# A decode layer on one core: the last PSUM copy and the output store moved to ScalarE

## The chip, the core and the metric

The kernel runs on one NeuronCore of a Trainium2 chip. The metric is the device time of one execution in microseconds (us), the lower the better. The core has five engines with instruction streams of their own: TensorE (PE in the profile, its weight loads PEld), VectorE (DVE), ScalarE (ACT), GpSimd (POOL) and SyncE (SP). SyncE and ScalarE both issue DMA transfers here; a transfer is issued by the engine's sequencer and then carried out by 16 DMA engines that all queues share. `ACTq` and `SPq` in the profile mean the sequencer of ScalarE and of SyncE.

## The reference

One decode step (batch 4, one token each) of a pre-norm transformer layer: attention over the last 2048 positions of a cache, then a gated MLP, both with residuals. Cut to what matters:

```python
# x: 4 x 1 x 1024; k_cache, v_cache: 4 x 4 x 8192 x 128; bf16 throughout
h  = x + attention(layernorm(x), k_cache, v_cache, wq, wo)   # 32 query heads, 4 kv heads
n  = layernorm(h)
h2 = h + (silu(n @ w1) * (n @ w3)) @ w2                      # 1024 -> 3584 -> 1024
return h2                                                    # 4 x 1 x 1024, bf16
```

## The kernel before

All weights and the cache go through one DMA queue, issued from SyncE in the order of use, into five rotating buffers. `w2` comes last, its second half in pieces of 5, 4, 2 and 1 rows, so that little work is left when the last byte arrives. The output is summed in one PSUM tile `y2_ps` of 128 partitions x 256 columns (fp32). Only 16 of its partitions are wanted: `JG` = 4 column blocks times 4 batch rows, `RS` = 8 partitions apart. The end of the kernel is a strict chain:

```python
    # SyncE has issued the last piece of w2 long before
    for i in range(IF):                                   # 28 row blocks of w2
        for j in range(JG):
            nc.tensor.matmul(
                y2_ps[QD * j : QD * (j + 1), :],
                lhsT=hgT[:, i, :],
                rhs=loaded["w2"][i][:, j * CG : (j + 1) * CG],
                start=False, stop=(i == IF - 1), skip_group_check=True,
            )

    res = act.tile([P, CG], BF16)
    nc.vector.tensor_copy(out=res[:], in_=y2_ps[:])                   # L440
    nc.sync.dma_start(                                                # L441
        out=out_flat.rearrange("b (j c) -> j b c", j=JG), in_=res[0:P:RS, :])
```

After this SyncE waits until all transfers have landed, one semaphore after another, and a barrier of all engines closes the program.

ScalarE's other DMA work are five small loads at the start: `x_sb` (4 rows of 1024) and four pieces of `x_q` (4 rows of 256).

## Time and profile before

The kernel before took 138.77 us (median of 3 runs, 138.73 to 138.95). The profiled execution's span, from first to last instruction, was 136.8 us.

| what | value | where it is read |
|---|---|---|
| HBM read | 55.59 MB, 406 GB/s over the span | HBM line of the page |
| DMA engines busy 90% or more | slices 2 to 36 of 40 | page, part 2 |
| last piece of `w2` landed | 133.11 us | chain of waits |
| last copy (VectorE) | 0.42 us | timeline |
| issue of the store (SyncE) | 0.69 us | timeline |
| wait for its landing (SyncE) | 1.1 us | waits of SyncE |

The page, kernel before. In the slice lines each digit is the busy share of a fortieth of the span, in tenths:

```profile
DMA  5999999999999999999999999999999999998950
...
HBM read 55.59 MB, written 0.01 MB: 406 GB/s over the span
```

So the kernel is bound by its stream of data for nearly the whole span, and what comes after 133 us is a tail that nothing overlaps.

The end of the chain that ended last, kernel before (start in us, duration in us, what):

```profile
95.73 37.38 DMA t<-in_B_w_dram
133.11 0.04 issue
133.15 0.32 PE y_ps L430 x4
133.49 0.42 DVE res L440
```

The timeline of the end, kernel before (start in us, duration in us, engine, line, operation, and in brackets the idle time before it and what ended it):

```profile
133.15 0.29 PE L430 MATMUL y_ps<-t,hgT 128*32 128x256 bf16 x4 [0.26 <-DMA t<-in_B_w_dram]
...
133.49 0.42 DVE L440 CAST res<-y_ps 128x256 bf16<-128x256 f32 x1 [11.29 <-PE y_ps L430]
133.94 0.69 SPq L441 DMA_DIRECT2D out_dram<-res  x1
```

The waits of SyncE at the end, kernel before (who waited for whom: total us, times, longest us). The store's landing takes 1.1 us after its issue:

```profile
SPq L467 <- DMA out_dram<-res: 1.1, 1, 1.1
```

The copies that ScalarE made before, in the groups of instructions (line, engine, operation, tiles, shapes, count, then busy us and mean ns of one):

```profile
L267 ACT COPY kT<-kt_ps 128x1024 bf16<-128x1024 bf16 x16 | 15.8, 1014 | 12.0 <-PE kt_ps L261 12.0
...
L318 ACT COPY bc<-bc_ps 128x128 f32<-128x128 f32 x1 | 0.3, 265 | 1.2 <-PE bc_ps L314 1.2
```

### The profile page before, as it was taken

Reading aid. Unit: us, or ns where it says so; the run is one execution under the profiler, and the core shown is the slowest. Engines: PE = TensorE matmul, PEld = TensorE weight load, DVE = VectorE, ACT = ScalarE, POOL = GpSimd, SP = SyncE. Lnnn points to the kernel's source line nnn. Section 1 sums busy time; section 2 is a strip of 40 time slices with the busy share of each in tenths; the row PEclk is TensorE's granted clock in tenths of the full one; section 3 lists DMA queues with packets and bytes.
Section 4 is the critical chain, followed back from the end, with each engine's and each line's share of the span. In section 5 each row is a group of like instructions: output and inputs, shape, how many; then the busy total and the mean of one; then the engine's idle time right before and its main releaser. Section 6 shows DMA issues by size and latency. Waiting matters only on the chain.

```text
span 136.8 us, 2307 instructions
## 1 busy us (share of the span) xinstructions
PE 68.3 (50%) x1035; PEld 42.3 (31%) x1035; DVE 43.0 (31%) x74; ACT 30.6 (22%) x35; POOL 1.7 (1%) x8
## 2 busy tenths in 40 slices
PE   0152303698989899105259259825080530802950
PEld 0110001274756565000149247602030210301820
DVE  6440000244444444709940030260004970170001
ACT  0400000155555646092943000000015000000000
POOL 5000000000000000000000000000000000000000
PEclk9999999999999999965555865896555586555586
DMA  5999999999999999999999999999999999998950
GB/s 156 441 418 503 402 393 441 421 431 436 421 431 421 436 436 417 433 445 469 450 421 402 407 427 441 453 441 402 427 449 453 411 419 424 450 460 364 418 219 2
DMA packets 3237, 55.74 MB, mean 407 GB/s; under 512 B 376, under 2 KB 408, under 8 KB 668
## 3 DMA queue, kind: packets, MB, share of 16 engines
q1 hardware_dynamic: 3188, 55.58, 95.2%
q8 instruction: 8, 0.13, 0.3%
q10 hardware_dynamic: 40, 0.02, 0.1%
q14 instruction: 1, 0.01, 0.0%
HBM read 55.59 MB, written 0.01 MB: 406 GB/s over the span
## 4 chain that ended last, share of the span: by engine, by line
DMA 43%; PE 29%; ACT 13%; DVE 8%; issue 4%; SPq 1%; ACTq 0%; DVEq 0%
DMA t<-in_B_w_dram 27%; DMA t<-in_A_wq_dram 15%; PE kt_ps L261 9%; ACT kT L267 6%; PE scores_ps L246 5%; PE OT_ps L324 5%; PE y_ps L351 4%; ACT z L302 3%; PE q_ps L213 2%; DVE rmax L278 2%; PE g_ps L400 2%; ACT Pm L283 2%; SPq L95 1%; DVE pT L292 1%; DVE z L298 1%
## 5 line engine op out<-in xcount | busy, mean ns | idle before, releaser
L267 ACT COPY kT<-kt_ps 128x1024 bf16<-128x1024 bf16 x16 | 15.8, 1014 | 12.0 <-PE kt_ps L261 12.0
L261 PE MATMUL kt_ps<-ident,t 128*128 128x128 bf16 x256 | 16.5, 220 | 0.0
L261 PEld LDWEIGHTS <-t 128*128 128x128 bf16 x256 | 14.4, 98 | 5.0 <-issue 4.9
L265 DVE COPY kT<-kt_ps 128x1024 bf16<-128x1024 bf16 x16 | 11.1, 692 | 15.2 <-PE kt_ps L261 15.2
L213 PE MATMUL q_ps<-t,xnT 128*4 128x512 bf16 x64 | 6.9, 596 | 11.9 <-DMA t<-in_A_wq_dram 11.9
L400 PEld LDWEIGHTS <-hnT 128*32 128x32 bf16 x128 | 4.9, 129 | 23.7 <-issue 20.8
L400 PE MATMUL u_ps<-t,hnT 128*32 128x448 bf16 x64 | 6.3, 573 | 10.9 <-DMA t<-in_B_w_dram 10.9
L246 PE MATMUL scores_ps<-kT,qz 128*32 128x512 bf16 x64 | 9.9, 609 | 3.1 <-ACT kT L267 2.9
L324 PE MATMUL OT_ps<-z,t 128*128 128x32 bf16 x256 | 7.5, 186 | 7.7 <-ACT z L302 5.0
L430 PE MATMUL y_ps<-t,hgT 128*32 128x256 bf16 x112 | 6.0, 384 | 8.1 <-DMA t<-in_B_w_dram 8.1
L324 PEld LDWEIGHTS <-t 128*128 128x128 bf16 x256 | 7.3, 102 | 8.4 <-issue 8.3
L400 PE MATMUL g_ps<-t,hnT 128*32 128x448 bf16 x64 | 5.2, 490 | 6.9 <-DMA t<-in_B_w_dram 4.6
L430 PEld LDWEIGHTS <-hgT 128*32 128x32 bf16 x112 | 4.6, 134 | 10.1 <-issue 5.8
L213 PEld LDWEIGHTS <-xnT 128*4 128x4 bf16 x64 | 2.0, 112 | 16.4 <-issue 16.0
L351 PE MATMUL y_ps<-t,o 128*32 128x256 bf16 x128 | 5.9, 372 | 0.8 <-DVE o L340 0.8
L223 DVE TENSOR_SCALAR q_sb<-q_ps 128x512 bf16<-128x512 f32 x1 | 0.7, 692 | 17.4 <-PE q_ps L213 17.4
L302 ACT ACTIVATE z<-pt_ps,mask 128x512 bf16<-128x512 f32 x8 | 5.3, 687 | 3.5 <-DVE z L298 3.5
L298 DVE TENSOR_SCALAR z<-pt_ps,mask 128x512 bf16<-128x512 f32 x8 | 5.5, 741 | 1.1 <-ACT z L302 0.8
L294 PE MATMUL pt_ps<-pT,perm 128*128 128x512 bf16 x4 | 2.4, 609 | 6.8 <-DVE pT L292 6.8
L414 DVE RECIPROCAL eg<-eg 128x896 f32<-128x896 f32 x1 | 5.8, 5752 | 0.0
L351 PEld LDWEIGHTS <-o 128*32 128x32 bf16 x128 | 4.4, 133 | 3.1 <-DVE o L340 1.9
L224 ACT ACTIVATE q_sb<-q_ps 128x512 bf16<-128x512 f32 x1 | 0.6, 597 | 21.1 <-DVE q_sb L223 21.1
(73 smaller groups left out, 40.3 us busy)
## 6 DMA issues: line engine op xcount, KB each, us to landing
t<-in_B_w_dram SPq DMA_DIRECT2D x4, 3584.0 KB
t<-in_A_k_cache_dram SPq DMA_DIRECT2D x4, 2048.0 KB, 25.4
t<-in_A_v_cache_dram SPq DMA_DIRECT2D x4, 2048.0 KB, 41.5
t<-in_A_wo_dram SPq DMA_DIRECT2D x2, 4096.0 KB, 42.2
t<-in_A_wq_dram SPq DMA_DIRECT2D x2, 2048.0 KB, 9.6
t<-in_A_wq_dram SPq DMA_DIRECT2D x1, 4096.0 KB, 21.0
t<-in_B_w_dram SPq DMA_DIRECT2D x1, 4096.0 KB, 37.7
t<-in_B_w_dram SPq DMA_DIRECT2D x1, 1280.0 KB, 34.4
```

Of the source, the lines that this page charges most:

```text
L213: nc.tensor.matmul(q_ps[QD * g : QD * g + B, hf * 512 : (hf + 1) * 512], lhsT=xnT[:, kc, :], rhs=wq_t[:, c0 : c0 + 512], start=(kc == 0), ...
L246: nc.tensor.matmul(scores_ps[QD * g : QD * (g + 1), n * 512 : (n + 1) * 512], lhsT=qz[:, b, g * QD : (g + 1) * QD], rhs=kT_v[:, g, :, :], ...
L261: nc.tensor.transpose(out=kt_ps[:, jj, :], in_=k_v[:, n * NJ + t * TB + jj, :], identity=ident[:])
L265: nc.vector.tensor_copy(out=kT[:, t * TB : (t + 1) * TB, :], in_=kt_ps[:])
L267: nc.scalar.copy(out=kT[:, t * TB : (t + 1) * TB, :], in_=kt_ps[:])
L298: nc.vector.tensor_scalar(out=z[:, :, g, :], in0=pt_ps[:], scalar1=mask[:, g : g + 1], scalar2=None, op0=ALU.mult)
L302: nc.scalar.mul(out=z[:, :, g, :], in_=pt_ps[:], mul=mask[:, g : g + 1])
L324: nc.tensor.matmul(OT_ps[:, b, :], lhsT=loaded["v"][b][:, j, :], rhs=PTz[j // NJ][:, (j % NJ) * B + b, :, :], start=(j == 0), stop=(j == J ...
L351: nc.tensor.matmul(y_ps[QD * j : QD * (j + 1), :], lhsT=o4[:, i, :, :].rearrange("p b s -> p (b s)"), rhs=loaded["wo"][i][:, j * CG : (j + ...
L400: nc.tensor.matmul(out_ps[QD * j : QD * (j + 1), hf, :HF], lhsT=hnT[:, k, :], rhs=loaded[kind][k][:, c0 : c0 + HF], start=(k == 0), stop=( ...
L414: nc.vector.reciprocal(out=eg[:], in_=eg[:])
L430: nc.tensor.matmul(y2_ps[QD * j : QD * (j + 1), :], lhsT=hgT[:, i, :], rhs=loaded["w2"][i][:, j * CG : (j + 1) * CG], start=False, stop=(i ...
```

## The change

VectorE and SyncE are replaced by ScalarE for both links of the chain: ScalarE's copy and its own queue should save a handover between engines, and perhaps time in the copy or the issue.

```diff
     res = act.tile([P, CG], BF16)
-    nc.vector.tensor_copy(out=res[:], in_=y2_ps[:])
-    nc.sync.dma_start(out=out_flat.rearrange("b (j c) -> j b c", j=JG), in_=res[0:P:RS, :])
+    nc.scalar.copy(out=res[:], in_=y2_ps[:])
+    nc.scalar.dma_start(out=out_flat.rearrange("b (j c) -> j b c", j=JG), in_=res[0:P:RS, :])
```

## The prediction

> **What bounds the kernel.** It streams 55.6 MB from HBM through one queue: the page's 40 slices show the DMA engines at 90% or more from the 2nd slice to the 36th, 406 GB/s over the 136.8 us span (HBM line). The chain of waits gives DMA 43%, PE 29%. It ends: last w2 piece lands 133.11; four matmuls to 133.47; the last copy on VectorE 133.49 to 133.91 (0.42 us); the store issued by SyncE 133.94 to 134.63 (0.69 us, timeline of the last 4 us); SyncE waits 1.1 us for the store to land (its own waits), to about 135.8; the closing barrier takes the remaining 1 us. The change touches only copy and issue, 1.1 us or 0.8% of the time, all on the critical path. The instruction order of the two builds differs only in these two instructions, which move to the end of ScalarE; no activation-table load is added.
>
> **Costs.**
> 1. Copy. VectorE's 128x256 fp32-to-bf16 copy took 425 ns. ScalarE took 265 ns to copy 128x128 and 1014 ns for 128x1024, so 0.836 ns per column, about 370 ns here (estimate). The Trainium skill, "ScalarE: Activation LUTs", What ACT_TABLE_LOAD costs, gives 186 + 0.833 N, 399 ns; this trace's 597 ns at 512 columns lies 15 ns below it. I take 380 ns: 0.045 us saved.
> 2. Handover from PE to the copy and from the copy to the store: VectorE to SyncE took 0.02 to 0.03 us. In the build the store still waits on a semaphore of the copy, so sharing an engine removes no handover. About 0.
> 3. Issue. The 4x4x256 store took SyncE 695 ns. ScalarE took 569 to 679 ns (median 583) for its small loads at the start, SyncE about 490 ns for its first loads. So ScalarE's sequencer may be up to 0.09 us slower per issue (estimate; the shapes differ). I take 730 ns: 0.035 us lost.
> 4. Transfer. The Trainium skill, "DMA: Bandwidth & Descriptors", Issuing engines are not separate DMA queues, says that the issuing engine changes only sequencer time, since all queues run on the same 16 DMA engines. SyncE's queue has drained by 133.1 and its sequencer stood waiting for VectorE, so there is nothing to jump ahead of. Landing stays 1.1 us, the barrier 1 us.
>
> ScalarE is idle from 104.5 us on and VectorE from 122.2, so the move frees no engine that anything waits for.
>
> Sum: -0.045 + 0.035 = -0.01 us, against the 2.8 us of 2%. Predicted 138.8 us, range 138.3 to 139.2 (the runs before spread 0.2 us; the issue adds to it). Chances: faster 0.01, within 2% 0.98, slower 0.01.
>
> **What the profile would show.**
> - Timeline: one ScalarE 128x256 copy of about 0.38 us right after the last matmul; a store on ScalarE's queue of 0.6 to 0.8 us, starting within 0.05 us of the copy's end. From last matmul to span end 3.3 to 3.5 us (3.36 before).
> - Waits: SyncE still waits for the store's landing; no new table load on ScalarE.
> - DMA view: 8 KB move from SyncE's queue (q1) to ScalarE's (q10); GB/s slices alike.
>
> **What would make it wrong.** A table load before the copy (1.28 us each in this trace); an issue by the long-idle ScalarE sequencer well over 0.8 us; a store that takes longer to land from the other queue; a copy whose completion its own sequencer sees late. None alone leaves the 2% band. Only a change of the stream could, and nothing before 133 us changes.

## The result, and the profile after

The changed kernel took 138.59 us (median of 4 runs, 138.54 to 138.65) against 138.75 us (4 runs, 138.61 to 138.95) of the kernel before. The ratio was 0.9987 with a 95% interval of 0.9973 to 1.0001: within 2%, and at the edge of being measurable at all. A second measurement (the run after_again below) gave 0.9988. Ratios are the mean time of one kernel's fast runs over that of the other's in the same rounds, so not quite the ratios of the medians quoted.

The page (part 2 and HBM line) and then the timeline of the end of the changed kernel:

```profile
DMA  5999999999999999999999999999999999998950
...
HBM read 55.59 MB, written 0.01 MB: 406 GB/s over the span
```

```profile
133.14 0.41 PE L430 MATMUL y_ps<-t,hgT 128*32 128x256 bf16 x4 [0.24 <-DMA t<-in_B_w_dram]
...
133.59 0.37 ACT L440 CAST res<-y_ps 128x256 bf16<-128x256 f32 x1 [28.90 <-PE y_ps L430]
133.99 0.61 ACTq L441 DMA_DIRECT2D out_dram<-res  x1
```

The stream is the same. In the tail the copy fell from 425 to 373 ns and the issue from 695 to 608 ns. And yet both spans are 136.8 us. The first line tells why: the last four matmuls, which the change does not touch, took 0.41 us in this execution and 0.29 us in the one before, because the granted TensorE clock differed at that moment (of the twelve other traces, five had a clock of 1.00 during these matmuls and 0.29 us, five 0.50 and 0.40 to 0.41 us, two lay between). The half microsecond around them, first of the kernel before and then of the changed one (stretch and its length in us, then busy time and count of PE, PEld, DVE, ACT and POOL, the granted clock, DMA share, GB/s):

```profile
133.10:133.60 0.50, 0.29 (x4) 0.10 (x3) 0.11 (x1) 0.00 (x0) 0.00 (x0) 1.00 0.00 0
```

```profile
133.10:133.60 0.50, 0.41 (x4) 0.11 (x3) 0.00 (x0) 0.01 (x1) 0.00 (x0) 0.54 0.00 0
```

The clock was 1.00 in one and 0.54 in the other. It is not the change that did this: in the run after_again the changed kernel had 1.00 there, its last matmuls ended 0.36 us after the last landing as in the kernel before, and its span was 136.7 us. That chance of 0.11 us is larger than the gain. So a comparison of spans would have said "nothing", and a comparison of the tail from the end of the matmuls says 0.09 us: from that point to the span's end it is 3.365 us before and 3.273 us after. The end of the chain of waits of the changed kernel has ScalarE's copy in the place of VectorE's:

```profile
97.19 35.91 DMA t<-in_B_w_dram
133.09 0.04 issue
133.14 0.43 PE y_ps L430 x4
133.59 0.37 ACT res L440
```

The waits of SyncE in the changed kernel. It now waits for the store of ScalarE, which is the only thing that it still has to do, so the wait is long and says nothing:

```profile
SPq L467 <- DMA out_dram<-res: 38.1, 1, 38.1
```

The 8 KB of the store moved between the queues. DMA view, kernel before and then after (packets, MB, share of time):

```profile
q1 hardware_dynamic: 3188, 55.58, 95.2%
...
q10 hardware_dynamic: 40, 0.02, 0.1%
```

```profile
q1 hardware_dynamic: 3168, 55.58, 95.2%
...
q10 hardware_dynamic: 60, 0.02, 0.1%
```

### The profile page after: what moved, and what is told of

Read it like the earlier page. It is cut to its first block, busy times and chain, and to the rows that moved or that the text cites. A ratio compares the mean times of both kernels' runs of the same rounds, so it can differ in the third digit from the quotient of the medians.

```text
span 136.8 us, 2307 instructions
## 1 busy us (share of the span) xinstructions
PE 70.0 (51%) x1035; PEld 43.7 (32%) x1035; DVE 42.5 (31%) x73; ACT 31.1 (23%) x36; POOL 1.7 (1%) x8
## 4 chain that ended last, share of the span: by engine, by line
DMA 42%; PE 31%; ACT 12%; DVE 8%; issue 3%; SPq 1%; ACTq 0%; DVEq 0%
DMA t<-in_B_w_dram 26%; DMA t<-in_A_wq_dram 15%; PE kt_ps L261 10%; ACT kT L267 5%; PE scores_ps L246 5%; PE OT_ps L324 5%; PE y_ps L351 5%; ACT z L302 3%; PE q_ps L213 3%; DVE rmax L278 2%; ACT Pm L283 2%; SPq L95 1%; DVE pT L292 1%; PE g_ps L400 1%; DVE z L298 1%
## 5 line engine op out<-in xcount | busy, mean ns | idle before, releaser
L261 PE MATMUL kt_ps<-ident,t 128*128 128x128 bf16 x256 | 17.7, 229 | 0.0
L261 PEld LDWEIGHTS <-t 128*128 128x128 bf16 x256 | 15.7, 103 | 4.9 <-issue 4.9
L324 PEld LDWEIGHTS <-t 128*128 128x128 bf16 x256 | 7.4, 105 | 8.3 <-issue 8.3
```

The costliest lines, as they stand in the source:

```text
L261: nc.tensor.transpose(out=kt_ps[:, jj, :], in_=k_v[:, n * NJ + t * TB + jj, :], identity=ident[:])
L324: nc.tensor.matmul(OT_ps[:, b, :], lhsT=loaded["v"][b][:, j, :], rhs=PTz[j // NJ][:, (j % NJ) * B + b, :, :], start=(j == 0), stop=(j == J ...
```

## The experiments

The tail was cut into pieces at the records of the trace: the last matmul's semaphore increment (22 to 24 ns after the end of its record), copy, issue, first packet of the store on the DMA engines, landing (the last semaphore increment of the store), end of span. One execution each, in ns; the first two rows are the two kernels, the others are the experiments below. The last column is the sum, less the issue, which overlaps the next column.

| kernel | to copy | copy | to issue | issue | issue start to first packet | first packet to landing | landing to span end | sum |
|---|---|---|---|---|---|---|---|---|
| before | 23 | 425 | 28 | 695 | 1294 | 503 | 1092 | 3365 |
| after | 22 | 373 | 30 | 608 | 1251 | 500 | 1097 | 3273 |
| after_again | 23 | 373 | 29 | 610 | 1252 | 503 | 1093 | 3273 |
| copy_only | 24 | 372 | 25 | 690 | 1288 | 499 | 1323 | 3531 |
| store_only | 23 | 425 | 32 | 600 | 1241 | 506 | 1099 | 3326 |
| before_plus_one | 24 | 424 | 27 | 690 | 1290 | 500 | 1330 | 3595 |
| copy_only_plus_two | 23 | 373 | 25 | 687 | 1288 | 496 | 1091 | 3296 |
| warm_sync_store | 23 | 425 | 28 | 584 | 1214 | 502 | 1022 | 3214 |
| warm_scalar_store | 23 | 372 | 30 | 544 | 1187 | 488 | 961 | 3061 |

Each piece repeats between executions: the copy within 2 ns on each engine, first packet to landing within 18 ns, and issue start to first packet within 14 ns for SyncE's first store (1288 to 1302 ns, but 1265 in swap_load_queues) and 12 ns for ScalarE's (1241 to 1253), the first stores of the chains below included. So differences of 40 ns here are readable, which the whole time with its spread of 0.2 to 0.4 us does not allow.

Theory A, formed from the two traces: the copy is 0.05 us shorter on ScalarE, and the store's first packet leaves 0.04 us sooner after the issue starts there. Theory B: the prediction's terms hold (copy -0.045, issue +0.035) and the two traces mislead. Theory C: it is chance.

### The tail sixteen times over

To lift 0.1 us above the noise, the copy and store were repeated 16 times in a chain, each copy waiting for the landing of the store before. Four kernels on one chip, in all four combinations of engines:

```diff
-    nc.vector.tensor_copy(out=res[:], in_=y2_ps[:])
-    nc.sync.dma_start(out=out_flat.rearrange("b (j c) -> j b c", j=JG), in_=res[0:P:RS, :])
+    for _ in range(16):
+        nc.vector.tensor_copy(out=res[:], in_=y2_ps[:])        # or nc.scalar.copy
+        nc.sync.dma_start(out=..., in_=res[0:P:RS, :])         # or nc.scalar.dma_start
```

tail16_dve_sp (VectorE copy, SyncE store):

> The closing copy and store of the kernel before (VectorE copy, SyncE store) made 16 times in a chain, each round waiting for the landing of the last. In the trace before, the copy's start to the last landing took 2.25 us; with 0.02 us to the next copy, 15 more rounds add about 34.1 us, so about 172.9 us. Both theories agree here; this is the base for the three others.

tail16_act_act (both on ScalarE):

> The same chain with the changed kernel's copy and store (both on ScalarE). Theory A, from the two traces: each round is 0.09 to 0.1 us shorter (copy -0.052, issue to first packet -0.043), so about 1.4 us under tail16_dve_sp, about 0.8%. Theory B, the terms of the prediction (copy -0.045, issue +0.035): 0.15 us under it. Theory C, that the difference in the two traces is one execution's chance: no steady difference in either term.

tail16_act_sp (ScalarE copy, SyncE store):

> ScalarE copy, SyncE store, 16 times. A and B agree on the copy: 0.7 to 0.8 us under tail16_dve_sp. A says that it stays 0.6 us over tail16_act_act, B that it is 0.5 us below tail16_act_act.

tail16_dve_act (VectorE copy, ScalarE store):

> VectorE copy, ScalarE store, 16 times. A: 0.6 us under tail16_dve_sp (15 x 0.043). B: 0.5 us over it (15 x 0.035). The sign decides the issue term.

Measured, medians of 4 runs each, beside 138.78 us for the kernel before (7 runs), with the pieces of one round as medians of the last 15 rounds of the profiled execution, in ns:

| run | time, us | copy | to issue | issue | issue start to first packet | first packet to landing | landing to next copy |
|---|---|---|---|---|---|---|---|
| tail16_dve_sp | 172.08 | 425 | 28 | 533 | 1171 | 496 | 92 |
| tail16_act_sp | 171.17 | 372 | 26 | 533 | 1172 | 491 | 77 |
| tail16_dve_act | 172.30 | 425 | 32 | 543 | 1187 | 491 | 92 |
| tail16_act_act | 170.32 | 372 | 30 | 544 | 1186 | 493 | 22 |

The copy term is confirmed: 53 ns between the medians, and no copy of any round was more than 2 ns off its median. So it is not chance (theory C). The issue term is not what either theory said. Theory A expected tail16_dve_act 0.6 us below the base and theory B 0.5 us above it; it was 0.22 us above, about 15 times the 16 ns that lie between 1171 and 1187 ns to the first packet. So once a few stores have gone out, ScalarE is the slower of the two by 14 to 16 ns, not the faster by 43.

The view by tile shows it: minimum, median and maximum of 16 stores, in ns. The first store of each chain is the maximum, as in the kernels themselves, and the others are far below. For tail16_dve_sp, tail16_act_sp, tail16_dve_act and tail16_act_act:

```profile
L442 SPq DMA_DIRECT2D out_dram<-res x16: 532/533/699, 134.1 to 167.4; - x16
```

```profile
L442 SPq DMA_DIRECT2D out_dram<-res x16: 533/533/698, 133.9 to 166.4; - x16
```

```profile
L442 ACTq DMA_DIRECT2D out_dram<-res x16: 543/543/606, 134.2 to 167.9; - x16
```

```profile
L442 ACTq DMA_DIRECT2D out_dram<-res x16: 543/544/609, 134.0 to 165.7; - x16
```

SyncE falls from 699 to 533 ns, ScalarE only from 609 to 544. (The second stores of the chains, in the trace, took 585 and 591 ns on SyncE and 593 on ScalarE.) What theory A took for a property of the queue is the cost of the first store, and that is larger on SyncE.

One more point, so that nobody reads the sum as the gain of the change: tail16_act_act lies 1.76 us below the base, which is more than A's 1.4. Of this, about 15 x 70 ns are the last column. In tail16_act_act the copy follows the landing by 22 ns; in the three others a separate semaphore instruction stands before each copy in the trace, because the copy waits for two things. This belongs to the chain and not to the kernels, which have one copy only. It is also why tail16_act_sp lay 0.85 us over tail16_act_act: that looks like theory A's 0.6 us, but about 15 x 55 ns of it are this column. And the base itself missed its expected 172.9 us by 0.8, because the later stores reach their first packet 123 ns sooner than the first one and the next copy starts 72 ns later than was assumed.

### Each half of the change alone

after_again (the changed kernel once more, 5 runs):

> The changed kernel again, in more rounds, to narrow the interval. Theory A (copy -0.05, issue to first packet -0.04): 0.1 us under the kernel before, ratio 0.9993. Theory B, the prediction's terms: 0.01 us under, ratio 0.9999. Theory C, chance: no difference.

copy_only:

```diff
-    nc.vector.tensor_copy(out=res[:], in_=y2_ps[:])
+    nc.scalar.copy(out=res[:], in_=y2_ps[:])
```

> The copy on ScalarE, the store still on SyncE. A and B: 0.05 us under the kernel before. In the trace: a ScalarE copy of about 0.37 us, then an issue on SyncE of about 0.695 us. If the issue record follows the copy's engine and not the queue, it would be about 0.61 us here.

store_only:

```diff
-    nc.sync.dma_start(out=out_flat.rearrange("b (j c) -> j b c", j=JG), in_=res[0:P:RS, :])
+    nc.scalar.dma_start(out=out_flat.rearrange("b (j c) -> j b c", j=JG), in_=res[0:P:RS, :])
```

> The copy on VectorE, the store on ScalarE. A: 0.04 us under the kernel before, issue record about 0.61 us. B: 0.035 us over it, issue record about 0.73 us. Both lie inside the noise of the whole time, so the trace decides: copy's end to first packet of the store 1.32 us before, 1.28 us by A.

Measured beside 138.79 us for the kernel before (9 runs): after_again 138.67 (ratio 0.9988, 0.9976 to 1.0001; as whole times these two do not rule out chance, but its trace repeats the pieces of the changed kernel within 4 ns), store_only 138.77 (0.9999, 0.9985 to 1.0013), copy_only 138.88 (1.0008, 0.9995 to 1.002). In the table of pieces the store on ScalarE has its first packet at 1241 ns instead of 1294, the copy its 372 ns; both halves do in the trace what theory A said for a single store. The issue record goes by the queue, not by the copy's engine.

But copy_only as a whole came out 0.09 us above the kernel before instead of 0.05 below, a difference inside the noise that its trace nevertheless has. Its table row says where: not in the copy, but 0.23 us between landing and span end. The instructions of the closing line, ScalarE's drain (count, duration in ns as minimum/median/maximum, first and last start in us), kernel before and copy_only:

```profile
L467 ACTq DRAIN  x2: 14/1098/2181, 102.3 to 136.4; - x2
```

```profile
L467 ACTq DRAIN  x2: 133/268/403, 133.7 to 136.8; - x2
```

In the kernel before the last drain starts at 136.4 us and takes 14 ns. In copy_only it starts at 136.8, takes 133 ns and holds up the barrier, although ScalarE had nothing to do since its copy.

### What delays the drain

before_plus_one (one useless ScalarE copy in the middle of the MLP, where ScalarE is idle; the kernel is otherwise that of before):

```diff
     gate_up("w3", u_ps)
+    scratch = act.tile([P, 1], FP32)
+    for k in range(1):
+        nc.scalar.copy(out=scratch[:, k : k + 1], in_=gs[:, 0, k : k + 1])
```

> Copy_only measured 0.09 us over the kernel before although its copy to landing was shorter; its trace shows ScalarE's closing drain 0.4 us late, at the barrier. Theory P: the delay comes from where ScalarE's instruction stream stands (65 recorded instructions in copy_only, 64 before, 67 after), not from the copy. Then the kernel before with one small ScalarE copy added at about 112 us, which nothing waits for, also shows a late ScalarE drain and ends about 0.2 us later, 138.95 to 139.0 us. Theory Q, the late drain belongs to a ScalarE copy at the very end with the store elsewhere: no late drain here, 138.79 us.

copy_only_plus_two (copy_only with two of them):

> copy_only with two such small ScalarE copies, so as many ScalarE instructions as the changed kernel. Theory P: no late drain, landing to span end 1.10 us instead of 1.32, and 138.7 us, 0.15 to 0.2 under copy_only. Theory Q: 138.88 us as copy_only.

Measured beside 138.69 us for the kernel before (9 runs): before_plus_one 138.90 us, ratio 1.0018 (1.0006 to 1.0031), the only single-tail kernel here that is clear of the noise; copy_only_plus_two 138.71 us (0.9999, 0.9987 to 1.0012). The drains of the closing line, before_plus_one and copy_only_plus_two:

```profile
L470 ACTq DRAIN  x2: 130/174/219, 112.1 to 136.8; - x2
```

```profile
L470 ACTq DRAIN  x2: 14/208/403, 133.5 to 136.3; - x2
```

Theory P holds: one instruction more on ScalarE, 25 us before the end and off every chain, costs 0.2 us at the barrier, and two more in copy_only take the delay away (landing to span end 1091 ns). With 65 recorded ScalarE instructions there was a late drain in both kernels; in none of the twelve other traces kept here was there one (62, 64, 66, 67, 71 and, in the chains, 64 and 95 to 104). Each is one profile, but the five timed runs of before_plus_one agree. What happens inside is not shown. A fetch of instructions is the obvious suspect. Against it speaks that the closing 8 KB fetch (queue q14) starts only after the drain in both late cases (137.49 us in copy_only, 137.47 us in before_plus_one). For it speaks that this fetch moves with the count in the kernels with one tail: its packet starts 0.62 to 1.04 us after the span's end with 62 and 64 instructions, 0.30 to 0.33 us after it with 65, and before the last drain with 66 and more. So the cause stays open; what is shown is that it goes by the number of instructions in ScalarE's stream. The changed kernel has 67 and is not hit.

### Why the issue estimate had the wrong sign

swap_load_queues gives the two first weight loads (128 rows) to ScalarE and the four `x_q` loads (4 rows) to SyncE:

```diff
     def load_rows(src, n, r0, pieces):
+        q = nc.scalar if src is wq_v and r0 == 0 else nc.sync
...
-            nc.sync.dma_start(
+            q.dma_start(
...
-        nc.scalar.dma_start(
+        nc.sync.dma_start(
             out=x_q[QD * j : QD * (j + 1) : RS, :], ...
```

> Why ScalarE's sequencer looked slower in the prediction. The two first weight loads (128 rows) go out from ScalarE, the four small x loads (4 rows) from SyncE. If the issue time goes by engine, as the prediction took it, ScalarE needs about 0.58 us for the weight loads and SyncE about 0.49 us for the small ones. If it goes by the transfer's form (4 rows or 128 rows), it is the other way round: about 0.49 us on ScalarE for the weights, 0.58 us or more on SyncE for the small loads.

One look, state unknown, 139.18 us; only the issue records count. Issues by line in that run (duration in ns as minimum/median/maximum):

```profile
L95 ACTq DMA_DIRECT2D t<-in_A_wq_dram x2: 367/406/444, 1.3 to 1.7; - x2
```

```profile
L146 SPq DMA_DIRECT2D x_q<-in_A_x_dram x4: 577/638/766, 1.1 to 27.9; - x4
```

The same two lines in the kernel before, where the engines were the other way round (the third of SyncE's three loads, 573 ns, has twice the size, but that is not what it shows: over all runs the same load took 383 to 955 ns, while the first two took 366 to 417):

```profile
L95 SPq DMA_DIRECT2D t<-in_A_wq_dram x3: 386/407/573, 0.7 to 1.6; - x3
```

```profile
L146 ACTq DMA_DIRECT2D x_q<-in_A_x_dram x4: 583/585/679, 1.4 to 3.3; - x4
```

The times stayed with the form of the transfer when the engines were swapped. These 4-row loads are dear and the first two 128-row loads cheap on both engines. The number of rows is not all of it: the cache loads, 128 rows out of a source of more dimensions, took SyncE 534 to 642 ns in the kernel before.

### Stores of the same form issued earlier

warm_sync_store (the kernel before, with one store of the same form from SyncE at 91.8 us; it writes other values, which the last store overwrites):

```diff
+    nc.sync.dma_start(out=out_flat.rearrange("b (j c) -> j b c", j=JG), in_=hn[0:P:RS, :])
     hnT = act.tile([P, KC, QD], BF16)
```

> The kernel before with one store of the same form issued from SyncE at about 92 us, four loads and 38 us of waiting before the last one. If it is the first store of its form that makes SyncE need 695 ns, the last issue falls to 530 to 630 ns and the kernel before gains up to 0.1 us, so most of the issue gain of the change was SyncE's first-time cost. If only recency counts, 690 to 700 ns again.

warm_scalar_store (the changed kernel, with two such stores from ScalarE at 120.4 and 127.9 us):

```diff
     nc.vector.tensor_tensor(out=hg[:], in0=u_ps[:, :, :HF], in1=gs[:], op=ALU.mult)
+    for _ in range(2):
+        nc.scalar.dma_start(
+            out=out_flat.rearrange("b (j c) -> j b c", j=JG), in_=hg[0:P:RS, 0, 0:CG]
+        )
```

> The changed kernel with two stores of the same form issued from ScalarE at about 120 us and 123 us (they write other values to the output, which the last store overwrites). In the chains ScalarE's issue fell from 609 ns at the first to 543 from the third on, SyncE's from 699 to 533. Theory W (recent stores of this form make an issue cheaper): last issue 545 to 595 ns, landing 0.03 to 0.065 us earlier; 138.6 us if nothing else changes. Theory X (the time to the first packet depends on how long the queue has been silent, or on the stream): about 608 ns again.

Measured beside 138.69 us for the kernel before (9 runs): warm_sync_store 138.53 us (0.999, 0.9978 to 1.0003), warm_scalar_store 138.49 us (0.9986, 0.9973 to 1.0). The last store, in the timeline of each:

```profile
133.89 0.58 SPq L442 DMA_DIRECT2D out_dram<-res  x1
```

```profile
134.06 0.54 ACTq L445 DMA_DIRECT2D out_dram<-res  x1
```

And the early store of warm_sync_store, which now is the first of its form:

```profile
L387 SPq DMA_DIRECT2D out_dram<-hn x1: 687/687/687, 91.8 to 91.8; - x1
```

SyncE's first store of this form took 687 ns here, in the middle of the kernel, as it took 687 to 699 at the end of the others. Its second took 584 ns, even after four loads and then 34 us without an issue; the third to sixteenth in the chain took 533. ScalarE's went 609, 590, 544. So the dear thing is being the first such store on a sequencer, not having been idle. What has to be the same is not separated: the early stores shared form, direction and target with the last one. A new source alone does not do it: SyncE's first load from `wo` took 337 ns and its first from the MLP's weights 328, much as the next ones did (333 and 328). Why ScalarE's first is cheaper is not tested; it had issued 4-row loads at the start, SyncE none, and in swap_load_queues, where SyncE had issued them, its last store took 630 ns instead of 695, which fits but is one record.

Both kernels save a little more after the landing: 1022 and 961 ns to the span's end instead of 1092. SyncE waits for five pairs of semaphores in turn at the end, 61 to 69 ns apart in the records, and the added transfers move the store's semaphore from the first place to the second or third. The waits ahead of it are then done while the store is still under way.

warm_scalar_store has the shortest tail of all, 0.30 us under the kernel before by its trace and 0.20 us by the medians, but its interval still touches 1. It was not timed against the changed kernel on one chip, so no more can be claimed than that it is not slower. Its two extra stores write wrong intermediate values to the output for some microseconds, for a gain of a seventh of a per cent; the plain change is the better kernel to keep.

## Why the prediction was right or wrong

- **Bound by the stream, tail of 3.4 us, 1.1 us of it touched.** Right. The same 406 GB/s in both kernels, and all differences lie after the last matmul.
- **Step 1, the copy, -0.045 us.** Right; 425 to 373 ns, -0.052, and 53 ns at the median of the chains. The line through two sizes in the trace (265 ns at 128 columns, 1014 at 1024, shown above) gave 370 ns, closer than the estimate of 399 ns from the formula of the Trainium skill in "ScalarE: Activation LUTs", What ACT_TABLE_LOAD costs, which is stated there for an ACTIVATE and not for a copy.
- **Step 2, the handover, about 0.** Right; 28 ns from VectorE's copy to SyncE's issue, 30 ns from ScalarE's copy to its own. Being on one engine saved nothing. In the chain it did, where a separate semaphore instruction before the copy fell away (77 to 22 ns).
- **Step 3, the issue, +0.035 us.** Wrong in sign: the record fell by 87 ns, and the first packet left 43 ns sooner. The step that failed is "ScalarE's sequencer may be up to 0.09 us slower per issue (estimate; the shapes differ)". It compared 4-row loads on ScalarE with 128-row loads on SyncE, so it measured the form of the transfer and took it for the engine, and its "about 490 ns" was a third of the 1.47 us that the timeline gives for SyncE's first three issues with the gaps between them; their records are 386, 407 and 573 ns. swap_load_queues shows that the form decides. What decides in the change is that the last store is SyncE's first of its kind, 687 to 699 ns, and ScalarE's first costs 600 to 610. Between warmed sequencers ScalarE is the slower one, by 14 to 16 ns to the first packet.
- **Step 4, the transfer unchanged.** Right; first packet to landing 503 and 500 ns. The Trainium skill says in "DMA: Bandwidth & Descriptors", Issuing engines are not separate DMA queues, that transfers run on the same 16 DMA engines whichever engine started them; the two figures agree with this.
- **Sum -0.01 us, 138.8 us.** The time lay in the range, but a range of 0.9 us cannot tell a wrong issue term from a right one, so the hit says nothing for step 3; as far as that step goes, it was luck. The sum should have been -0.09 us by the trace, and 0.12 and 0.16 us were measured by the two pairs of medians. The expected "3.3 to 3.5 us" from last matmul to span end was missed by 0.03 us at the lower edge (3.273), for the same reason.
- **What would make it wrong.** The list had the right kinds of thing but not the one that occurs: a late drain on ScalarE worth 0.23 us, which a single instruction more or less switches on and off. The changed kernel was lucky in this; half of the change alone was not.

## What to carry to other kernels

Take the issue cost of a DMA only from a transfer of the same form in the trace, and look whether it was the first such store on that sequencer; here that was worth 103 to 166 ns of the issue record on SyncE, more than the choice of the engine (87 ns). When a change is worth 0.1 us, compare pieces of the tail between fixed points or repeat the tail in a chain; the spans of two executions differed by as much through the clock of four matmuls, and by twice as much through the place of one instruction in a stream. Moving 1.1 us of work in a tail behind a stream of 133 us cannot matter much: count what share of the time the touched links have before anything else.

## What the Trainium skill lacked or had wrong

- "DMA: Bandwidth & Descriptors": no cost of one issue from SyncE or ScalarE by form is given for this chip. Measured over all runs: 327 to 444 ns for 128-row weight loads (but 383 to 955 for the third one of the kernel), 534 to 686 ns for the cache loads, 554 to 766 ns for 4-row loads, 687 to 699 ns for SyncE's first 4x4x256 store (630 in the one run where SyncE had issued 4-row loads) and 533 ns from the third on, 600 to 610 and 543 ns on ScalarE.
- "DMA: Bandwidth & Descriptors", Specifications, gives about 0.6 us to the first byte for this path. From the start of the issue record it was 1.17 to 1.30 us; 0.6 us fits only if it is counted from the end of the issue record (599 ns before, 643 ns after).
- "ScalarE: Activation LUTs", What ACT_TABLE_LOAD costs: the section has no formula for a copy out of PSUM. The one for an ACTIVATE with immediate scale and bias, 186 + 0.833 N, would give 399 ns for 256 columns (estimate); the copy from PSUM to SBUF took 372 to 373 ns in all runs. So it is 26 ns too high for this copy, and 28 ns at 128 columns (265 ns).
- "DMA: Bandwidth & Descriptors", Rules for kernel authors, names a VectorE copy as the way out of PSUM. This is incomplete rather than wrong: for fp32 to bf16 at 256 columns ScalarE's copy was the faster one, 373 against 425 ns.
- "Runtime: NRT & Kernel Launch", Instruction fetch mechanics, calls the cost of crossing a boundary between fetched blocks mostly hidden. No page explains a drain that comes 0.4 us late and costs 0.23 us with 65 recorded ScalarE instructions and not with 64, 66 or 67. No run here shows that it is a fetch, so it is not shown that the page is wrong.
